# First four token tiles of an MLP layer in float32 on TensorE, and a new order of the start

## The chip, the cores and the metric

The kernel runs on one core of a Trainium2 chip. The metric is the device time of one execution in microseconds. TensorE (PE) multiplies matrices into PSUM, VectorE (DVE), ScalarE (ACT) and GpSimd (POOL) compute element by element, SyncE (SP) mostly issues transfers (DMA). Each engine works through its own queue in order.

## The reference

x is 2048 x 576 in float32, w1 576 x 4608, w2 4608 x 576. The result is the sum of x, a Fourier mixing of its layer norm, and a two-layer MLP of the same layer norm:

```python
xn = _layernorm(x, axis=-1)
# A: a = xn @ dft_hid_re.T ; b = xn @ dft_hid_im.T ; y = dft_seq_re @ a - dft_seq_im @ b
# B: h = maximum(xn @ w1, 0) ; y = h @ w2
return x + _A_ref(xn, A_dft_seq_re, A_dft_seq_im, A_dft_hid_re, A_dft_hid_im) + _B_ref(xn, B_w1, B_w2)
```

## The kernel before, in words

Tokens come in 16 tiles of 128, four to a group (`g` 0 to 3). The 4608 hidden features come in 9 blocks of 512; a block has two halves of w1 and of w2 (`i` 0 and 1), a half two slices of 128 features (`f`). TensorE works in f16: every float32 operand is split into a high f16 part and a low f16 remainder, and a product is made of high*high, high*low and low*high. From block 1 on, and in the Fourier part, products also go by a scheme of seven block products in place of eight; block 0 is plain.

The program has three stages: the MLP blocks 0 to 8, a transform along the hidden axis, and one along the sequence. Nothing is left to a scheduler: strings of words (`BLOCK0`, `BLOCK1`, `BLOCK`, ...) give the order, each word is one step for one engine, and within an engine the steps run in the order of their words. This document is on the start, block 0, whose words are:

- `lx:t` loads x tile t (L350), `lw:i` a half of w2 (L354), `load_w1_main` and `load_w1_rest` a half of w1 (L366, and L377 with L378), issued by SP or ScalarE. At most eight such transfers are under way: each takes one of eight semaphores in turn.
- `bn:t` and `ag:t`: row statistics of tile t on VectorE (L473, L477); `sq:a:b` on ScalarE and `ch:a:b` on VectorE: the factors of tiles a to b (L482, L489 to L493).
- `hi:t`: the high f16 part of the normalised tile into one of seven staging slots (ScalarE, L512 and L515); `xn:t`: the normalised tile in float32, in place, by ScalarE (`A`, L532) or VectorE (`V`, L534); `lo:t`: the low part (VectorE, or GpSimd `G`, L520 and L521); `T:t`: the staged tile transposed into `xT` by a transposing DMA that SP issues (L542).
- `th`, `tl`, `ch_`, `cl`: for tiles 0 and 1, the same transpose in f16 on TensorE (L553) with copies out of PSUM by ScalarE (L1114, L1115).
- Powers of two as scales: `ms` (ScalarE, L904) or `mx` (VectorE, L887) takes a maximum of w1; `pa` multiplies it across the partitions (TensorE, L434), `pb` reduces (VectorE, L437), `pc` spreads it (TensorE, L443), `pd` makes the scale (VectorE, L446 to L451). `sw`, `qm`, `qa` to `qd` do that for w2.
- `wh:f` and `wl:f`: high and low parts of w1 for two passes (ScalarE L921, VectorE L926 and L927); `uh`, `ul` the same for w2 (L1016, L1020).
- `p:t:i` (and `p0`): the first layer for tile t and half i, 28 f16 matmuls of 128 columns (L588), into a PSUM bank per slice. `f:n`: n idle matmuls (L1075).
- `oa`, `od`: ReLU, high part on ScalarE (L603), low on VectorE (L611). `m:g:k`: the second layer of block 0 for group g (TensorE, L850). `e`, `ad`: eviction and the transfer to DRAM. `P:g:f`: the first layer for a whole group g of 512 columns (L588).
- `ts`, `tu`, `tv`, `tw`: differences of tiles for the later blocks. `nx`, `na` to `nd`, `nh`, `nl`, `ns`: scale and split w1 of block 1.

The lines that a sentence can't say are the order of the start and the words' meaning in `act`:

```python
"th": lambda t: transposes_pe(t, HI, Q[0]), "tl": lambda t: transposes_pe(t, LO, Q[1]),
"p0": lambda f: piece(0, (f,), WK0), "p": lambda t, i: piece(t, (2 * i, 2 * i + 1)),
```

## Time and profile before

| | |
|---|---|
| median of 3 runs | 1224.66 us (1223.04 to 1225.59) |
| profiled execution | 1223.44 us |
| its span | 1221.7 us |
| TensorE busy | 1213.3 us, 99% of the span |
| VectorE, ScalarE, GpSimd busy | 1043.4, 726.5, 210.6 us |
| mean DMA rate | 144 GB/s |

Rows of the view in order of time have the start in us from the span's start, the length, the engine, the line, the operation, what is written and read, and a count; in brackets the engine's idle time just before and what ended it. In the view of groups a row ends with the busy time in us, the mean ns of one, and the idle time before. The view of stretches gives for each stretch its length, the busy time of PE, PEld (weight loads), DVE, ACT and POOL with counts, the granted TensorE clock, the busy share of the DMA engines and GB/s. The view of waits names who waited for whom: total us, times, longest. The 1.7 us between the span and the execution's time lie outside what the trace shows.

### The profile page before, as it was taken

The page shows a single profiled execution, that of the slowest core. Times are in us where ns is not written, and L with a number is a line of the kernel's source. Part 1 is how long each engine was busy: PE and PEld are TensorE (multiplying, and loading weights), DVE is VectorE, ACT ScalarE, POOL GpSimd, SP SyncE. Part 2 cuts the span into 40 slices and gives each one's busy share as a digit, 9 for nine tenths or more (in the row PEclk, how much of TensorE's full clock was granted, in tenths as well). Part 3 has the DMA queues.
Part 4 walks back from the last instruction along what each step waited for, and adds up shares of the span by engine and source line. Part 5 has one row for each costly group of instructions (what it writes and reads, how often), then busy time and mean ns, then how long its engine had stood idle before and what let it go on. Part 6 is the DMA issues. An engine that isn't in the chain of part 4 may idle for free.

```text
span 1221.7 us, 26201 instructions
## 1 busy us (share of the span) xinstructions
PE 1213.3 (99%) x10516; PEld 999.8 (82%) x10516; DVE 1043.4 (85%) x2004; ACT 726.5 (59%) x1251; POOL 210.6 (17%) x274
## 2 busy tenths in 40 slices
...
GB/s 234 227 170 197 158 133 181 148 155 151 164 140 169 152 146 175 134 144 150 148 120 153 140 186 166 113 98 66 157 150 136 134 79 47 92 158 182 141 133 35
DMA packets 127050, 175.97 MB, mean 144 GB/s; under 512 B 48336, under 2 KB 88784, under 8 KB 126928
## 3 DMA queue, kind: packets, MB, share of 16 engines
...
q10 hardware_dynamic: 560, 0.39, 0.1%
...
## 4 chain that ended last, share of the span: by engine, by line
PE 99%; DMA 1%; DVE 0%; POOL 0%; issue 0%; ACT 0%
PE bank L713 28%; PE bank L1483 27%; PE p L810 27%; PE bank L1397 8%; PE p L588 4%; PE p L850 4%; PE p L1075 1%; DMA raw_w<-in_w_dram 0%; DMA accs<-in_x_dram 0%; DVE st L473 0%; PE p L553 0%; DVE row L440 0%; POOL dbuf L521 0%; DVE o L1495 0%; PE p L434 0%
## 5 line engine op out<-in xcount | busy, mean ns | idle before, releaser
L810 PE MATMUL p<-w2s,h 128*128 128x288 f16 x2688 | 357.9, 286 | 0.0
L1483 PE MATMUL bank<-R,cs 128*128 128x288 f16 x2688 | 330.3, 286 | 0.0
L1483 PEld LDWEIGHTS <-cs 128*128 128x128 f16 x2688 | 263.0, 98 | 66.3
L810 PEld LDWEIGHTS <-h 128*128 128x128 f16 x2688 | 263.0, 98 | 61.7
L713 PEld LDWEIGHTS <-dbuf 128*128 128x128 f16 x1568 | 153.3, 98 | 21.1 <-issue 0.8
L713 PEld LDWEIGHTS <-wbuf 128*128 128x128 f16 x1568 | 153.4, 98 | 20.2
L1016 ACT ACTIVATE cs<-tb,sc_c 128x1024 f16<-128x1024 f32 x56 | 63.7, 1147 | 89.2 <-PE bank L1483 61.7
L713 PE MATMUL bank<-xT,wbuf 128*128 128x256 f16 x896 | 110.7, 273 | 0.0
L713 PE MATMUL bank<-xT,dbuf 128*128 128x256 f16 x896 | 110.2, 273 | 0.0
L835 POOL DMA_DIRECT2D spill<-dbuf x70 | 62.4, 933 | 159.5 <-DVE dbuf L828 117.0
L1020 DVE SCALAR_TENSOR_TENSOR cs<-tb,sc_c,cs 128x1024 f16<-128x1024 f32 x56 | 71.5, 1282 | 20.3 <-ACT cs L1016 19.6
L713 PE MATMUL bank<-accs,wbuf 128*128 128x256 f16 x672 | 86.9, 273 | 0.0
L713 PE MATMUL bank<-accs,dbuf 128*128 128x256 f16 x672 | 86.1, 273 | 0.0
L760 DVE TENSOR_TENSOR h<-s,h 128x1024 f16<-128x1024 f32 x64 | 77.4, 1217 | 1.7 <-ACT h L754 1.7
L1016 ACT ACTIVATE cs<-accs,sc_c 128x1024 f16<-128x1024 f32 x40 | 45.8, 1147 | 55.2 <-PE bank L1483 41.7
L754 ACT ACTIVATE h<-s 128x1024 f16<-128x1024 f32 x64 | 66.5, 1050 | 12.3 <-DVE s L751 12.3
L1246 ACT ACTIVATE f<-f 128x1024 f32<-128x1024 f32 x64 | 67.1, 1049 | 1.4 <-DMA f<-in_cre_dram 1.3
L835 POOL DMA_DIRECT2D spill<-wbuf x42 | 39.6, 942 | 148.8 <-DVE wbuf L828 120.5
L722 ACT ACTIVATE h<-accs 128x256 f16<-128x256 f32 x128 | 50.9, 409 | 23.8 <-DVE accs L737 21.7
L1020 DVE SCALAR_TENSOR_TENSOR cs<-accs,sc_c,cs 128x1024 f16<-128x1024 f32 x40 | 51.1, 1282 | 13.0 <-ACT cs L1016 12.7
L703 ACT ACTIVATE accs<-bank 128x256 f32<-128x256 f32 x97 | 36.9, 380 | 41.1 <-PE bank L713 20.0
L824 ACT ACTIVATE dbuf<-p,c_ub 128x576 f32<-128x576 f32 x61 | 45.0, 737 | 25.4 <-PE p L810 25.4
...
## 6 DMA issues: line engine op xcount, KB each, us to landing
spill<-dbuf POOLq DMA_DIRECT2D x80, 288.0 KB, 4.6
...
spill<-wbuf POOLq DMA_DIRECT2D x48, 288.0 KB, 5.6
raw_w<-in_w_dram SPq DMA_DIRECT2D x18, 576.0 KB, 4.8
...
```

The costliest lines, as they stand in the source:

```text
L588: nc.tensor.matmul(ps[:, cols], w1s[b, i // 2][:, i % 2 * 2 + h, y], xT[g][:, h * KC + z, cols], start=(n == 0), stop=(n == len(wk) - 1),)
L713: nc.tensor.matmul(ps, l, r, start=first and m == 0, stop=m == len(todo) - 1, skip_group_check=not first,)
L722: nc.scalar.activation(next(high_low(q)), SOURCE[q], AF.Relu)
L754: order["s"] = nc.scalar.activation(next(high_low(SUMS)), stage_of(slice(1, 5)), AF.Copy).ins
L760: order["lo"] = nc.vector.tensor_tensor(lo, stage_of(slice(1, 5)), hi, ALU.subtract).ins
L810: nc.tensor.matmul(ps[:, c], h[:, x, qa, c * P : (c + 1) * P], w[:, y, qb], start=first and i == 0 and j == 0, stop=i == NQ - 1 and j == 2 ...
L835: nc.gpsimd.dma_start(spill[g, row, col], sums[g, row, col], accum_op=ALU.add)
L1016: nc.scalar.activation(hi, src, AF.Copy, scale=s)
L1020: nc.vector.scalar_tensor_tensor(lo, src, s, hi, ALU.mult, ALU.subtract)
L1246: nc.scalar.activation(f, f, AF.Abs, scale=2.0**-10, accum_out=sums_c[:, n, q : q + 1])
L1397: nc.tensor.matmul(ps, x[:, k, c * P : (c + 1) * P], dsp[z][:, a, y], start=first and m == 0, stop=m == len(PASSES) - 1, skip_group_check= ...
L1483: nc.tensor.matmul(ps, w[:, a, RANK[k]], r[:, c, RIGHT[rq]], start=first and k == 0 and j == 0, stop=k == HK - 1 and j == 2, skip_group_ch ...
```

## The change

**Float32 for tiles 0 to 3.** In block 0 the first layer of the first four tiles no longer uses split operands. `tf:t` transposes the normalised float32 tile on TensorE (five matmuls with a float32 identity), `cm:t` and `cr:t` copy the result out of PSUM (four parts of 128 rows, and the rest of 64), and `pf:t:i` multiplies the raw w1 half with it in float32: two slices of five matmuls. Since the raw w1 isn't scaled, `sf:i` multiplies the finished PSUM banks by the scale, in place, before the ReLU. `th`, `tl`, `ch_`, `cl` and `p0` are gone. Tiles 0 to 3 still go through `hi` or the new `hj` (the same from `xn`), `lo` and `T` for later blocks, later than before.

**w1 by fewer transfers.** A half of w1 now takes three transfers in place of five. The first half goes through ScalarE's queue alone, x tiles 0 to 3 through SP.

**Order and engines.** `BLOCK0` and `BLOCK1` are written in a new order; only the first 84 idle matmuls are left. Some steps can go by VectorE that were ScalarE's (`hi`, `oa`, `wh`, `tu`, `sf`), and staging slots are handed out in another order of tiles.

```diff
+    def transposes32(t, main, rest):
+        for k in range(KM):
+            nc.tensor.transpose(main[:, k * P : (k + 1) * P], xns[t][:, k * P : (k + 1) * P], ident32)
+        nc.tensor.transpose(rest[:REM], xns[t][:, KM * P :], ident32)
...
+    def piece32(t, i):
+        for r in range(2):
+            w = raws["w1", 0, i]
+            ps = banks0[0][2 * i + r][:, t * P : (t + 1) * P]
+            for k in range(KM):
+                h, q = divmod(k, 2)
+                nc.tensor.matmul(ps, w[:, 2 * r + h, q], xt32[:, t, k], start=k == 0, stop=False)
+            nc.tensor.matmul(ps, w[:REM, 2 * r, 2], xt32[:REM, t, KM], start=False, stop=True)
+
+    def scaled(i, eng=nc.scalar):
+        ps = XY[i]
+        s = sc["w1", 0][:, i : i + 1]
...
     load_x(0)
...
-    for half in range(2):
-        eng = (nc.sync, nc.scalar)[half]
-        load_w1_main(0, 0, slice(half, half + 1), eng)
-        load_w1_rest(0, 0, half, eng)
-    for t in range(1, TG):
+    load_w1_main(0, 0, nc.scalar)
+    load_x(1)
+    load_w1_rest(0, 0, nc.scalar)
+    for t in range(2, TG):
         load_x(t)
-    load_w1_main(0, 1, slice(0, 2))
-    for half in range(2):
-        load_w1_rest(0, 1, half)
+    load_w1_main(0, 1)
+    load_w1_rest(0, 1)
...
 BLOCK0 = """
-bn:0 ag:0 sq:0:0 ch:0:0 bn:1 bn:2 bn:3 ag:2 hi:0 xn:0:A ms:0 ag:1 lo:0:G f:79 th:0 ag:3 mc:0
+f:79 bn:0 ag:0 lw:0 sq:0:0 ch:0:0 f:5 lw:1 xn:0:A bn:1 tf:0 ag:1 bn:2 sq:1:1 ch:1:1 xn:1:V cr:0:V
```

**Where instructions moved.** SP's queue at the start of the program, before: `accs` are x tiles, `raw_w_0` the halves of w1, then `raw_w_0_0_376` the first half of w2, and transposes (`xT`) ahead of x tiles 8 and 10.

```order
L350 DMA accs<-in_x_dram 128x576 x3
L366 DMA raw_w_0_1_149<-in_w_dram 128x4x256
L377 DMA raw_w_0_1_149<-in_w_dram 96x2x128
L378 DMA raw_w_0_1_149<-in_w_dram 32x2x128
L377 DMA raw_w_0_1_149<-in_w_dram 96x2x128
L378 DMA raw_w_0_1_149<-in_w_dram 32x2x128
L350 DMA accs<-in_x_dram 128x576 x4
L354 DMA raw_w_0_0_376<-in_w_dram 128x1152
L542 DMA_TRANSPOSE xT_134<-dbuf 128x10x128 x2
L350 DMA accs<-in_x_dram 128x576 x2
L354 DMA raw_w_0_1_693<-in_w_dram 128x1152
```

The same place of the changed kernel; `raw_w_0_0_269` and `raw_w_0_1_282` are the halves of w2, the two `accs` behind them tiles 8 and 10.

```order
L350 DMA accs<-in_x_dram 128x576 x4
L366 DMA raw_w_0_1_154<-in_w_dram 128x4x256
L378 DMA raw_w_0_1_154<-in_w_dram 96x4x128
L378 DMA raw_w_0_1_154<-in_w_dram 32x4x128
L350 DMA accs<-in_x_dram 128x576 x4
L354 DMA raw_w_0_0_269<-in_w_dram 128x1152
L354 DMA raw_w_0_1_282<-in_w_dram 128x1152
L350 DMA accs<-in_x_dram 128x576 x2
```

The second half of w2 and tiles 8 and 10 moved ahead of all transposes, right behind the first half of w2.

VectorE's queue around the statistics of tile 10 in block 0, before: `st_567` holds tile 10's, `st_570` tile 8's; the rows ahead are the end of the last split of w1 (`wl:3`) and a difference of tiles.

```order
L926 SCALAR_TENSOR_TENSOR wbuf<-raw_w_0_1_149,c_sw_210,wbuf 128x2x256
L927 SCALAR_TENSOR_TENSOR wbuf<-raw_w_0_1_149,c_sw_210,wbuf 32x2x128
L655 TENSOR_TENSOR accs<-accs 128x2x256
L655 TENSOR_TENSOR accs<-accs 128x2x32
L520 TENSOR_TENSOR dbuf<-accs,dbuf 128x2x32
L521 TENSOR_TENSOR dbuf<-accs,dbuf 128x2x256
L473 BN_STATS st_567<-accs 128x6 x2
L473 BN_STATS st_570<-accs 128x6 x2
```

The same work in the changed kernel: `st_391` holds tile 10's statistics, the copy behind it is `cr:3`, the reduction `pb:1`, then four aggregates and the first split of w1 (`wl:0`).

```order
L485 BN_STATS st_383<-accs 128x6 x2
L485 BN_STATS st_386<-accs 128x6 x2
L485 BN_STATS st_391<-accs 128x6 x2
L588 COPY xT_137<-p_0_1_3_185 64x128
L439 TENSOR_REDUCE top<-p_0_1_2_184 1x1
L489 BN_AGGR mv<-st_356 128x2
L489 BN_AGGR mv<-st_352 128x2
L489 BN_AGGR mv<-st_383 128x2
L489 BN_AGGR mv<-st_386 128x2
L962 SCALAR_TENSOR_TENSOR wbuf<-raw_w_0_0_153,c_sw_316,wbuf 128x2x256
L963 SCALAR_TENSOR_TENSOR wbuf<-raw_w_0_0_153,c_sw_316,wbuf 32x2x128
```

Tile 10's statistics moved from behind the last split of w1 to ahead of the first one, and ahead of the second power's reduction.

TensorE's queue around `pc:1` in the changed kernel; `p_0_0_0_180` and `p_0_0_1_181` are the banks of group 0, L575 and L576 transpose in float32 (`tf:3`), L1112 and L1113 are the float32 matmuls, L445 is `pc:1`.

```order
L436 MATMUL p_0_1_2_184<-ident,mb_1_372 1x128
L575 MATMUL p_0_1_1_183<-xT_136,accs 128x128 x4
L576 MATMUL p_0_1_3_185<-xT_136,accs 64x128
L1112 MATMUL p_0_0_0_180<-xT_137,raw_w_0_0_153 128x128 x4
L1113 MATMUL p_0_0_0_180<-xT_137,raw_w_0_0_153 128x128
L1112 MATMUL p_0_0_0_180<-xT_137,raw_w_0_0_153 128x128 x4
L1113 MATMUL p_0_0_0_180<-xT_137,raw_w_0_0_153 128x128
L445 LDWEIGHTS ones
L445 MATMUL p_0_1_3_185<-top,ones 128x1
L1112 MATMUL p_0_0_1_181<-xT_137,raw_w_0_1_154 128x128 x4
L1113 MATMUL p_0_0_1_181<-xT_137,raw_w_0_1_154 128x128
```

Before, idle matmuls (L1075) stood on both sides of `pc:1`; now work of the first layer stands ahead of it and behind it.

233 lines of the change are left out of this document (131 added, 102 removed).

## The prediction

> **What bounds the kernel now.** I read the page first, then TensorE's waits after the start, then TensorE in order of time.
>
> ```profile
> PE 1213.3 (99%) x10516; PEld 999.8 (82%) x10516; DVE 1043.4 (85%) x2004; ACT 726.5 (59%) x1251; POOL 210.6 (17%) x274
> PE bank L443 <- DVE row L440: 0.7, 1, 0.7
> 21.03 1.11 PE L1075 MATMUL p<-dbuf 128*128 128x128 f16 x17
> 21.98 11.11 PE L588 MATMUL p<-xT,wbuf 128*128 128x128 f16 x196
> 34.94 12.68 PE L588 MATMUL p<-xT,wbuf 128*128 128x128 f16 x224
> 47.45 11.92 PE L850 MATMUL p<-w2s,h 128*128 128x288 f16 x96
> ```
>
> TensorE is busy all through, but its first 22 us are mostly idle matmuls (L1075, `f`). The first matmul that counts starts at 21.98: the pieces (`p`) of the first layer for tiles 0 to 7, in two lots of 224. One takes 12.68/224 = 56.6 ns, a `p` word of 28 takes 1.585 us. At 47.45 the second layer begins (`m:0:0`), and from there to the end TensorE waits once, 0.7 us (the second row, the only one that the view of waits gives for it after 47 us). So a microsecond gained or lost ahead of `m:0:0` comes out at the end in full. What the change is worth is the new start of `m:0:0` against 47.45, and what becomes of that one wait.
>
> **The change, part by part: TensorE's own work.** Removed: all idle matmuls but 84, 20 f16 transposes, and the 224 f16 pieces of tiles 0 to 3 (12.7 us). Added: 80 float32 matmuls and 20 float32 transposes of 128 columns. No row has a float32 matmul. The kernel itself makes float32 products out of f16 halves, and high and low of both operands give at most four f16 products; so I count passes of 56.6 ns. Bounds: one pass from below; from above four, each with its weight load in the open:
>
> ```profile
> L588 PEld LDWEIGHTS <-wbuf 128*128 128x128 f16 x441 | 24.7, 98 | 0.1
> ```
>
> 4 x (98 + 56.6) = 618 ns. I take four passes whose loads hide behind the matmuls, as every load of the pieces does now (98 ns each, yet one piece every 56.6): 4 x 56.6 = 226 ns, so 18.1 us in all. That is 5.4 us more than the f16 pieces, but it needs no split weights, no scale and no transposing DMA, so it can run in the first 22 us. The transposes cost 5 x 56.6 to 5 x 226 ns a tile, 0.3 to 1.1 us.
>
> **How early float32 can start.** ScalarE's rows of before give the prices:
>
> ```profile
> 6.56 0.81 ACT L512 ACTIVATE dbuf<-accs,sh,r 128x512 f16<-128x512 f32 x1 [1.01 <-DVE sh L493]
> 7.67 0.85 ACT L532 ACTIVATE first_xn<-accs,sh,r 128x576 f32<-128x576 f32 x1
> 8.42 1.47 ACT L904 ACTIVATE wbuf<-raw_w 128x1536 f16<-128x1536 f32 x1
> 34.94 1.08 ACT L603 ACTIVATE h<-p 128x512 f16<-128x512 f32 x2 [0.93 <-PE p L588]
> ```
>
> Tile 0's factor is known at 6.56 as before, `xn:0` takes 0.85 (to 7.4), then come a deviation and the maximum of w1's first half (L904, with its accumulator about 1.65) ahead of `cm:0` (0.58 from PSUM, by L603): 10.0. The transposes of tile 1 stand in between on TensorE, so `pf:0:0` starts at about 10.9. Were nothing else in the way, float32 would be over at 10.9 + 18.1 + 2 us for transposes and powers = 31, and `m:0:0` would start at 31 + 12.7 = 43.7, a gain of 3.7.
>
> **What is in the way: x tile 10.** The new order loads both halves of w2 and then x tiles 8 and 10 right behind tiles 4 to 7, and VectorE's queue now holds the statistics of tile 10 ahead of `cr:3` and `pb:1`. TensorE's `pc:1` needs `pb:1`, and fifty float32 matmuls (`pf:0:1`, `pf:1:1`, `pf:3:0`, `pf:2:1`, `pf:3:1`) stand behind `pc:1`. When does tile 10 land?
>
> ```profile
> L354 SPq DMA_DIRECT2D raw_w<-in_w_dram x1: 328/328/328, 13.0 to 13.0; - x1
> DMA to landing us min/median/max: 5.3/5.3/5.3
> accs<-in_x_dram SPq DMA_DIRECT2D x12, 288.0 KB, 4.4
> raw_w<-in_w_dram SPq DMA_DIRECT2D x2, 576.0 KB, 5.1
> 12.00:14.00 2.00, 1.32 (x20) 1.15 (x21) 1.33 (x3) 0.83 (x2) 0.63 (x1) 1.00 1.01 281
> 24.00:26.00 2.00, 2.00 (x40) 2.00 (x38) 2.00 (x6) 2.00 (x5) 0.00 (x0) 1.00 1.00 302
> 26.00:28.00 2.00, 2.00 (x39) 2.00 (x37) 2.00 (x6) 2.00 (x5) 0.28 (x1) 1.00 0.99 384
> ```
>
> Before, the first half of w2 landed at 13.0 + 5.3 = 18.3, behind tiles 0 to 7 and w1; the bytes up to there are the same now. The last two columns are the DMA engines' busy share and GB/s: with a share of about 1.0 they move 281 to 384, so fewer, larger transfers can win little (I take 0.6 us, bounds 0 and 1.0). Tile 10 has 576 + 2 x 288 KB more ahead of it, itself included: 1.18 MB, at 384 to 281 GB/s 3.1 to 4.2 us; at 343, the mean of the last two rows, 3.4. So 18.3 - 0.6 + 3.4 = 21.1, bounds 20.4 and 22.5.
>
> **From tile 10 to `m:0:0`, on VectorE.** Starts of neighbours in order of time give each price:
>
> ```profile
> 15.84 0.57 DVE L534 TENSOR_SCALAR accs<-accs,mv,r 128x576 f32<-128x576 f32 x1
> 16.32 1.53 DVE L473 BATCH_NORM_STATS2 st<-accs 128x6 f32<-128x288 f32 x4
> ...
> 20.69 0.13 DVE L446 TENSOR_SCALAR half<-p 128x1 f32<-128x1 f32 x1
> ...
> 20.98 0.20 DVE L477 BATCH_NORM_AGGREGATE mv<-st 128x2 f32<-128x12 f32 x1
> 21.10 0.70 DVE L926 SCALAR_TENSOR_TENSOR wbuf<-raw_w,c_sw,wbuf 128x512 f16<-128x512 f32 x1
> ...
> 22.11 0.73 DVE L926 SCALAR_TENSOR_TENSOR wbuf<-raw_w,c_sw,wbuf 128x512 f16<-128x512 f32 x1
> ...
> 23.17 0.16 DVE L489 RECIPROCAL r<-u 128x4 f32<-128x4 f32 x1
> ...
> 24.05 0.74 DVE L926 SCALAR_TENSOR_TENSOR wbuf<-raw_w,c_sw,wbuf 128x512 f16<-128x512 f32 x1
> ...
> 27.64 0.20 DVE L520 TENSOR_TENSOR dbuf<-accs,dbuf 128x64 f16<-128x64 f32 x1
> ...
> 28.37 1.52 DVE L473 BATCH_NORM_STATS2 st<-accs 128x6 f32<-128x288 f32 x4
> 29.82 0.20 DVE L520 TENSOR_TENSOR dbuf<-accs,dbuf 128x64 f16<-128x64 f32 x1
> ...
> 31.28 0.66 DVE L973 CAST mb<-c_mw 128x2 bf16<-128x2 f32 x1
> 31.85 0.20 DVE L477 BATCH_NORM_AGGREGATE mv<-st 128x2 f32<-128x12 f32 x1
> ...
> 32.65 0.39 DVE L477 BATCH_NORM_AGGREGATE mv<-st 128x2 f32<-128x12 f32 x3
> 33.27 0.28 DVE L437 TENSOR_REDUCE top<-p 2x1 f32<-2x128 f32 x1 [0.22 <-PE p L434]
> ...
> 33.72 0.21 DVE L520 TENSOR_TENSOR dbuf<-accs,dbuf 128x64 f16<-128x64 f32 x1
> 35.04 0.16 DVE L446 TENSOR_SCALAR half<-p 128x2 f32<-128x2 f32 x1 [0.52 <-PE p L443]
> ...
> 36.28 0.21 DVE L520 TENSOR_TENSOR wbuf<-first_xn,wbuf 128x64 f16<-128x64 f32 x1
> ```
>
> Between tile 10 and the end of `wl:1` (w1's last split, which `p:6:0` needs) VectorE's queue holds: five tiles' statistics at 1.45/2 = 0.73 (3.63); four `wl` at 1.01 (4.04); two `lo` at 0.73 (1.46); one `ch` 0.88; `pd` 0.29; `pb` 0.28; `qb` 0.45; `qd` 1.24; `qm` 0.57; eight aggregates at 0.13 (1.04); one `xn` 0.48; one copy out of PSUM without a row of its own, between the 0.28 of the reduction and the 0.57 of the wide row, nearer the small one: 0.3. Sum 14.7. For waits on TensorE and ScalarE in between I add 1.2 (an estimate; the rows show 0.22 and 0.52 for two of them; bounds 0.3 and 2). So `wl:1` ends at 21.1 + 14.7 + 1.2 = 37.0.
>
> TensorE meanwhile: `pc:1` at 21.1 + 0.73 + 0.3 + 0.28 + 0.2 of hops = 22.6, then 50 x 0.226 = 11.3, 0.4 for the powers of w2, and `p:4:1` 1.6: 35.9. It waits 1.1 for `wl:1`. Seven `p` words of 1.585 follow (11.1) and end at 48.1. The transposing DMAs of tiles 4 to 7 are needed at 34.3, 37.0, 41.7 and 43.3 and stay ahead by my count of ScalarE's queue, tile 4 narrowly. For `od:0:1`, last of VectorE's work for `m:0:0`, I allow 0.2 (0 to 1). `m:0:0` starts at 48.3, 0.85 later than 47.45.
>
> **Given back at 107 us.** That one wait hangs between two matmuls of w1's power:
>
> ```profile
> 105.80 0.94 PE L713 MATMUL bank<-accs,dbuf 128*128 128x256 f16 x7
> 107.47 0.16 PE L443 MATMUL bank<-row,ones 2*128 2x2 bf16 x1 [0.73 <-DVE row L440]
> ```
>
> Seven products stand between them now, fourteen in the new order. Another seven (0.94) cover 0.73: gain 0.73 (0 if VectorE is late there).
>
> **Costed at nothing.** w1 of later blocks comes in 3 transfers in place of 5, which takes work off SP; TensorE waits for no transfer after 47 us. The in-place scaling (`sf`) and the new engines for single steps work beside a busy TensorE; if that cover is gone after 47 us, a wait of 1 to 3 us would show there, and that is inside the slower chance.
>
> **Sum.** +0.85 - 0.73 = +0.1 us, on the profiled execution 1223.44 + 0.1 = 1223.5. The median shown lies 1.2 above that execution, so 1224.8. With the bounds of tile 10 (-0.7, +1.4), of the waits (-0.9, +0.8) and of `od` (-0.2, +0.8), not all at one end, the likeliest case by itself runs from 1223.2 to 1227.2. A measurement here can tell about 0.2%, 2.4 us.
>
> **Rivals.** *Slower: float32's weight loads don't hide.* The rows show a load of 98 ns that hides because the next one proceeds behind a matmul; none shows it for 4-byte weights. At one load of 98 a pass, a matmul takes 392 ns. Float32 then runs without a break: 10.9 + 80 x 0.392 + 1 for transposes and powers + 12.7 = 56.0, that is 8.5 later, less 0.73: 1232.5. With transposes at 392 too it is 1235. It decides from where 50 matmuls behind `pc:1` outlast VectorE: 1.1 us of slack / 50 = 22 ns more, 248 ns; at 300 ns the cost is 2.6. For it: idle TensorE time is what the plan spends. Against: two of four passes could share a load.
>
> [...]
>
> *Faster: tile 10 comes early.* If DMA keeps 384 GB/s from the start, tile 10 lands near 18 and VectorE, not waiting, ends `wl:1` 3 us sooner; TensorE's own sum (43.7) and ScalarE's queue then allow `m:0:0` at about 45.3: -2.2 - 0.73, 1221.8. Against it: the 281 to 302 GB/s at a busy share of 1.0.
>
> *It does nothing that it says:* float32 starts at 11 but TensorE stands at `pc:1` and `wl:1` for what it saved. That is my forecast.
>
> **Chances.** Forecast 0.52; slower 0.34 (loads 0.28, new waits after 47 us 0.06); faster 0.14. Range 1221.8 to 1235: left out are loads dearer than the rival's (0.1) and a little below. The forecast's own case gives 0.48 within 0.2%, 0.04 slower; the faster one 0.12 faster, 0.02 within; the slower 0.32 slower and 0.02 within. So faster 0.12, same 0.52, slower 0.36.
>
> **What would show it.** Right: float32 matmuls about 226 ns apart, VectorE idle ahead of tile 10's statistics for 2 to 4 us, landing near 21; TensorE waiting at `pc:1` for VectorE and at `p:6:0` for `wl:1`; `m:0:0` at 48.3; no wait near 107. Wrong: float32 over 250 ns apart, or `m:0:0` before 46, or new waits of TensorE after 50 us.

## The result, and the profile after

The changed kernel takes 1241.66 us (median of 4 runs, 1240.48 to 1242.73), the kernel before 1225.08 (4 runs, 1223.04 to 1225.59): the ratio is 1.0138, 95% interval 1.0121 to 1.0156. The forecast of 1224.8 with a range from 1221.8 to 1235 was wrong. The profiled execution has a span of 1240.0, against 1221.7.

TensorE's busy row of the page of the changed kernel:

```profile
PE 1222.1 (99%) x10294; PEld 1001.7 (81%) x10294; DVE 1056.2 (85%) x2026; ACT 723.0 (58%) x1244; POOL 215.6 (17%) x277
```

The share is the same 99%; it doesn't show what happened. TensorE in order of time does (start, length, line; idle time before it in brackets, with what ended it). In the changed kernel L883 is the second layer, L620 the first, L436 and L445 the matmuls of a power, L746 and L843 block 1's products and its second layer:

```profile
11.87 1.16 PE L1112 MATMUL p<-xT,raw_w 128*128 128x128 f32 x8 [0.68 <-ACT xT L586]
...
50.53 6.04 PE L883 MATMUL p<-w2s,h 128*128 128x288 f16 x48
59.46 8.98 PE L883 MATMUL p<-w2s,h 128*128 128x288 f16 x72 [2.88 <-DVE wbuf L896]
69.53 6.20 PE L620 MATMUL p<-xT,wbuf 128*128 128x512 f16 x28 [1.10 <-issue]
...
81.98 0.16 PE L445 MATMUL pm<-top,ones 1*128 1x1 bf16 x1 [2.82 <-DVE top L439]
82.07 4.44 PE L883 MATMUL p<-w2s,h 128*128 128x288 f16 x24
...
117.76 0.22 PE L436 MATMUL bank<-ident,mb 128*2 128x128 bf16 x1 [0.47 <-DVE mb L1009]
...
119.54 0.17 PE L445 MATMUL bank<-row,ones 2*128 2x2 bf16 x1
...
128.74 1.26 PE L746 MATMUL bank<-accs,dbuf 128*128 128x256 f16 x7 [2.16 <-DVE s L772]
129.79 4.48 PE L883 MATMUL p<-w2s,h 128*128 128x288 f16 x24
...
150.92 3.22 PE L746 MATMUL bank<-xT,dbuf 128*128 128x256 f16 x28 [0.95 <-DVE s L784]
153.98 3.10 PE L843 MATMUL p<-w2s,h 128*128 128x288 f16 x24
```

`m:0:0` starts at 50.53, 3.1 later, and behind it six waits stand where before had one of 0.73. The rows that answer to three of these places in the kernel before (L443 at the end of w1's power, L434 at the start of w2's power, L810, block 1's second layer; in the changed kernel they are the rows at 81.98, 117.76 and 153.98):

```profile
71.72 0.17 PE L443 MATMUL pm<-top,ones 1*128 1x1 bf16 x1
...
105.65 0.22 PE L434 MATMUL bank<-ident,mb 128*2 128x128 bf16 x1
...
136.78 1.63 PE L810 MATMUL p<-w2s,h 128*128 128x288 f16 x12
```

These four places cut the way into stretches. The table has them for the two kernels and for the runs on which the explanation rests; every number is a difference of two starts in that run's profile.

| run | `m:0:0` starts | to w1's power | to w2's power | to block 1's second layer | which starts |
|---|---|---|---|---|---|
| before | 47.45 | 24.3 | 33.9 | 31.1 | 136.78 |
| after | 50.53 | 31.5 | 35.8 | 36.2 | 153.98 |
| h_before_after | 49.88 | 24.5 | 35.5 | 36.1 | 145.96 |
| h_after_before_2 | 50.55 | 33.6 | 33.9 | 31.7 | 149.85 |
| no_sums_of_group_0 | 50.66 | 26.1 | 35.5 | 34.3 | 146.58 |
| chain_early | 50.46 | 26.2 | 35.1 | 36.3 | 148.02 |
| block_1_order_before | 52.02 | 30.9 | 35.5 | 31.4 | 149.73 |

Each profile is one execution. In the five runs below that leave every step up to `m:0:0` as it is in the changed kernel, TensorE's first wait for tile 1 is 1.50 to 3.19 us long, the granted clock from 8 to 25 us 0.80 to 1.00, and `m:0:0` starts between 50.55 and 53.69. So a run's stretches behind `m:0:0` have to be read apart from its time.

The loss at 154 us is 3.1 + 7.2 + 1.9 + 5.1 = 17.2; 1.1 more comes behind it (18.3 in all between the two spans; the medians differ by 16.6). Three pieces of it are not waits. 24 matmuls of L883 take 4.44 and 4.48 in place of 3.10, twice. And about 0.8 of the 5.1 is no loss at that place: one product more (seven matmuls of L746, 147 in place of 140) stands ahead of the first L843 now. The granted clock (the column of 0.85 to 1.00, behind TensorE's busy time) around 82 us:

```profile
80.00:82.00 2.00, 0.02 (x1) 0.85 1.13 213
82.00:86.50 4.50, 4.50 (x26) 0.69 1.07 224
86.50:90.00 3.50, 3.50 (x20) 1.00 0.63 122
```

A wait of 2.8 us is followed by 4.5 us at 0.69 of the clock: it costs 1.3 us again.

### The profile page after: what moved, and what is told of

It reads as the page before. It is cut to its first block, busy times and chain, and to the rows that moved or that the text cites. A ratio compares the mean times of both kernels' runs of the same rounds, so it can differ in the third digit from the quotient of the medians.

```text
span 1240.0 us, 25723 instructions
## 1 busy us (share of the span) xinstructions
PE 1222.1 (99%) x10294; PEld 1001.7 (81%) x10294; DVE 1056.2 (85%) x2026; ACT 723.0 (58%) x1244; POOL 215.6 (17%) x277
## 3 DMA queue, kind: packets, MB, share of 16 engines
q1 hardware_dynamic: 99216, 122.25, 33.9%
## 4 chain that ended last, share of the span: by engine, by line
PE 87%; DVE 7%; DMA 3%; ACT 1%; issue 1%; SPq 1%; POOL 0%; DVEq 0%; ACTq 0%; POOLq 0%
PE bank L1535 27%; PE bank L746 25%; PE p L843 25%; PE bank L1449 8%; DMA raw_w<-in_w_dram 1%; PE p L883 1%; DMA accs<-in_x_dram 1%; DVE w2s L1056 1%; DVE c_mf L920 1%; PE p L1112 1%; DMA xT<-wbuf 1%; SPq L699 0%; DVE h L759 0%; ACT dbuf L532 0%; DVE wbuf L542 0%
## 5 line engine op out<-in xcount | busy, mean ns | idle before, releaser
L843 PE MATMUL p<-w2s,h 128*128 128x288 f16 x2688 | 358.0, 286 | 0.4
L843 PEld LDWEIGHTS <-h 128*128 128x128 f16 x2688 | 262.9, 98 | 63.2 <-issue 1.3
L746 PEld LDWEIGHTS <-dbuf 128*128 128x128 f16 x1568 | 153.4, 98 | 23.5 <-issue 3.5
L746 PEld LDWEIGHTS <-wbuf 128*128 128x128 f16 x1568 | 153.4, 98 | 20.2
L746 PE MATMUL bank<-xT,wbuf 128*128 128x256 f16 x896 | 110.9, 273 | 0.0
L746 PE MATMUL bank<-xT,dbuf 128*128 128x256 f16 x896 | 109.9, 273 | 0.9 <-DVE s L784 0.9
L746 PE MATMUL bank<-accs,dbuf 128*128 128x256 f16 x672 | 86.8, 273 | 2.2 <-DVE s L772 2.2
L1056 DVE SCALAR_TENSOR_TENSOR cs<-tb,sc_c,cs 128x1024 f16<-128x1024 f32 x56 | 71.5, 1282 | 20.1 <-ACT cs L1052 19.8
L746 PE MATMUL bank<-accs,wbuf 128*128 128x256 f16 x672 | 86.9, 273 | 0.0
L1056 DVE SCALAR_TENSOR_TENSOR cs<-accs,sc_c,cs 128x1024 f16<-128x1024 f32 x40 | 51.1, 1283 | 13.3 <-ACT cs L1052 12.8
```

The source lines that it names most:

```text
L746: nc.tensor.matmul(ps, l, r, start=first and m == 0, stop=m == len(todo) - 1, skip_group_check=not first,)
L843: nc.tensor.matmul(ps[:, c], h[:, x, qa, c * P : (c + 1) * P], w[:, y, qb], start=first and i == 0 and j == 0, stop=i == NQ - 1 and j == 2 ...
L1056: nc.vector.scalar_tensor_tensor(lo, src, s, hi, ALU.mult, ALU.subtract)
```

## The experiments

**Which half of the new order costs?** The first four runs separate the start from what follows it.

```diff
 ... xn:11:A lo:8:V m:0:0
-m:0:1 ag:15 tv:0:0:V sq:12:15 ch:12:15 lo:11:G oa:1:1 tw:0:0 od:1:1 T:9 e:0:0:V ...
+tv:0:0:V tw:0:0 tu:0:2 ag:15 od:1:2 lo:11:G tv:0:2:V oa:1:1 m:0:1 e:0:0:V ...
```

> The changed kernel's steps up to and with m:0:0 (float32 start, new loads, new order), and from there on the remaining steps in the order and on the engines of before. Theory ORDER (the new order behind m:0:0 costs by itself): what is left of the loss is the later m:0:0, 50.53 against 47.45, so 1225.1 + 3.1 = 1228.2; eight steps that before had done by m:0:0 are still to be done, which may cost one short wait, so 1227.5 to 1231. TensorE stands still for under 2 us between 51 and 152 us (10.4 after the change) and its clock does not fall at 82 and at 129 us. Theory LATE (the waits come only because everything after the float32 stage starts 3 us late): the waits stay whatever the order, 1238 to 1242.

1241.39, ratio 1.0133 (1.0112 to 1.0154). It seemed to speak for LATE, but nearly all of TensorE's idle time was one wait: 8.2 us in front of `e:0:0`, behind a chain that I had put there myself (`tv:0:0`, its transposing transfer, `tu:0:2`, `tv:0:2`). The run was made again below.

The opposite half, on the kernel before:

```diff
 ... tv:0:2:V ag:13 oa:1:1 m:0:0
-m:0:1 e:0:0:V lo:8:V ts:1:1:V ...
+L1:0 L1:1 T:10 lo:8:V m:0:1 sq:12:15 ch:12:15 od:1:1 T:9 e:0:0:V ad:0:0 ...
```

> The other half: the steps of before up to and with m:0:0 (no float32, the old loads), and from there on the remaining steps in the changed kernel's order and on its engines. Theory ORDER: TensorE's idle time of 10.4 us between 50 and 152 us, less the 0.73 that before had, and about 3 us of lowered clock come back although nothing is late: 1225.1 + 10 to 14 = 1235 to 1239, with VectorE's eviction of m:0:0 waited for and the clock lowered near 79 and 126 us. Theory LATE: with m:0:0 at 47.45 the new order has the slack that it was written for, 1224.4 to 1227 (0.73 less for the filled wait at 107 us).

1230.07, ratio 1.0053 (1.0035 to 1.0071): between the two. Its profile on TensorE says where:

```profile
49.88 15.06 PE L858 MATMUL p<-w2s,h 128*128 128x288 f16 x120
...
74.34 0.17 PE L443 MATMUL pm<-top,ones 1*128 1x1 bf16 x1
...
121.04 1.65 PE L721 MATMUL bank<-accs,dbuf 128*128 128x256 f16 x7 [2.37 <-DVE s L747]
```

Behind the old start the new order has no wait from `m:0:0` up to w1's power; it has the wait of block 1 (2.37, against 2.16 in the changed kernel) in full. The stretch of +7.2 needs the new start, that of +5.1 does not. (This execution took 1234.79, the longest of six: its clock lay at 0.66 from 10 to 20 us, and `m:0:0` came 2.4 later than in the kernel before, with the same start.)

```diff
-... hi:14:V ... xn:15:A ... tu:1:1:V ... lo:14:V ... oa:2:0:V ... tu:1:2:V ... oa:2:2:V ... e:1:2:V ... oa:2:3:V ... tv:3:1:G
+... hi:14 ... xn:15:V ... tu:1:1 ... lo:14:G ... oa:2:0 ... tu:1:2 ... oa:2:2 ... e:1:2:A ... oa:2:3 ... tv:3:1:V
```

> The changed kernel with ten of its engine choices behind m:0:0 put back to those of before (tu:1:1, tu:1:2, oa:2:0, oa:2:2, oa:2:3, hi:14 and e:1:2 from VectorE to ScalarE, lo:14 to GpSimd, xn:15 and tv:3:1 to VectorE); the order stays. Theory ENGINES (VectorE is given steps that stand behind transposing transfers): the wait of 2.82 at 81.98 goes, and with it the fall of the clock that makes 24 matmuls take 4.44 in place of 3.10; the waits of 1.1 at 69.53 and of 2.16 at 128.74 may go too: 1241.7 - 2.8 - 1.3 = 1237.5, down to 1232 if all three go. Theory PLACES (the places of the steps in VectorE's row cost it, not the engines): 1240 to 1243.

The wait at 82 and the low clock behind it went (1.00 from 70 to 90 us), and block 1's second layer started 3.6 sooner in the profile (150.37); the time stayed at 1241.49 (ratio 1.0140, 1.0119 to 1.0161; runs from 1239.6 to 1244.2). The other waits stayed. So in this order that one wait hangs on the engines, but no change of the time is shown.

```diff
-            for k in range(KM):
+            for k in range(KM // 2):
```

> The changed kernel with two of the four full row blocks of w1 left out of its float32 products (6 matmuls of 10 are left in a pf; the first layer of tiles 0 to 3 is only partly computed). This takes 32 x 0.272 = 8.7 us out of TensorE's float32 stage, more than the 6 us by which it was dearer than forecast. Theory LATE: m:0:0 starts at 47.5 or before and the waits behind it go: 1225 or less. Theory ORDER: m:0:0 starts earlier by 1 to 4 us (VectorE ends wl:1 at 38.9 in the changed kernel, of which about 2 us were waits for TensorE's powers), but VectorE's row reaches e:0:0 at 56 to 58.6 whatever m:0:0 does, so the wait in front of it grows by what m:0:0 gains, and the other waits stay: 1237 to 1241.

1244.39, ratio 1.0155 (1.0131 to 1.0179). With 8.7 us of float32 gone, `m:0:0` started at 51.14, no sooner. TensorE first waited 2.5 us for tile 1 and then ran at half the clock until 25 us:

```profile
15.00:20.00 5.00, 5.00 (x20) 0.50 1.03 395
20.00:25.00 5.00, 5.00 (x19) 0.50 0.76 280
```

and later it waited 1.07 for the last split of w1, which VectorE ended at 41.1. Both theories failed on the size. With the clock at half, the run doesn't show what float32 alone costs; it shows that VectorE's row can bound `m:0:0` too.

**Single waits.** Four runs took one thing each out of the stretch behind the start.

```diff
-m:0:0 m:0:1 ag:15 tv:0:0:V sq:12:15 ch:12:15 lo:11:G oa:1:1 tw:0:0 od:1:1 T:9 e:0:0:V
+m:0:0 m:0:1 e:0:0:V ag:15 tv:0:0:V sq:12:15 ch:12:15 lo:11:G oa:1:1 tw:0:0 od:1:1 T:9
```

> The changed kernel with one step moved: VectorE's eviction e:0:0 from its place behind fifteen VectorE instructions to the place directly behind the issue of m:0:1. Theory QUEUE (the 2.88 at 59.46 is only the place of e:0:0 in VectorE's row): VectorE reaches it at 52.1, waits till m:0:0 is done at about 53.6, and frees the bank at 54.5, before TensorE needs it at 56.6: the wait goes, 1241.7 - 2.9 = 1238.8; the fifteen instructions behind it come 1 to 2.4 us later, so of the wait of 1.1 at 69.53 and 2.82 at 81.98 up to 2 may be added back: 1237.5 to 1241. Rival BACKLOG (VectorE has more work in this stretch than TensorE gives it time for; a step moved forward only moves the wait): the sum of TensorE's idle time from 50 to 100 stays at 6.8 to 7.5 and the time at 1241 to 1243.

1243.02 (1.0166, 1.0148 to 1.0184): the wait shrank to 0.31, and one of 3.10 for VectorE's `od` (L646) came at 71. So a wait did move, as BACKLOG says, though TensorE's idle time from 50 to 100 us fell to 3.8, from 6.8. The time doesn't tell the two apart: in the profile TensorE had waited 3.19 for tile 1, its clock lay at 0.54 from 10 to 15 us, and `m:0:0` started at 53.68, 3.2 later than in the changed kernel.

```diff
-... hj:0 bn:10 pa:1 ... qm:0 bn:8 pf:0:1
+... hj:0 pa:1 ... qm:0 bn:8 bn:10 pf:0:1
```

> The changed kernel with the statistics of tile 10 (bn:10) moved in VectorE's row from ahead of cr:3 and pb:1 to behind those of tile 8. VectorE waited 2.53 there for tile 10's transfer. Theory X10 (that wait pushes VectorE's whole row up to wl:1, m:0:0 and e:0:0): cr:3 and pb:1 come 2 to 2.5 earlier, wl:1 ends near 37 in place of 38.99, m:0:0 starts at 49 to 49.5 in place of 50.53, the wait at 59.46 falls from 2.88 to 1.5 to 2.4: 1241.7 - 1 to 2 = 1239.7 to 1240.7, at most 1238.5. Rival FLOAT32 (TensorE's own sum sets m:0:0): m:0:0 stays within 0.4 of 50.5 and the time at 1241 to 1242.5, whatever VectorE gains.

1245.00 (1.0172, 1.0153 to 1.0191), worse than either theory. TensorE's clock lay at 0.50 from 15 to 25 us in the profile, VectorE then waited 4.56 for the transposes of tile 3, and `m:0:0` started at 56.54. What tile 10 costs by itself stays open.

```diff
-lo:1:G ... lo:4:G ... lo:5:G ... lo:3:G ... lo:0:G ... lo:2:G ... ts:0:2:G ts:0:3:G ... lo:9:G ... lo:10:G ... ts:1:0:G ... lo:11:G
...
-        nc.gpsimd.memset(st[:, :, 2, RH : 2 * RH], 0.0)
+        nc.gpsimd.memset(st[:, :, 2:], 0.0)
```

> The changed kernel without the twelve steps (lo and ts) that GpSimd does ahead of e:0:0: the low halves of tiles 0 to 5 and 9 to 11 stay zero, and some sums of rows are left out, so that part of the product is missing. VectorE's row and places stay. Between 36 and 58.6 us nine VectorE instructions took longer than their like elsewhere, each beside a GpSimd instruction: L963 1.38 against 0.47, L1056 1.38 against 0.81, L503 1.01 against 0.16, L542 1.77 against 0.68, L541 1.06 and 0.71 against 0.20, L502 0.91 against 0.16: together 5.4 us. Theory SHARED (the two engines stand in each other's way): they take 0.47, 0.81, 0.16, 0.68, 0.20 and 0.16, wl:1 ends 0.9 sooner, VectorE reaches e:0:0 by 54, the wait at 59.46 goes and m:0:0 comes up to 0.9 earlier: 1241.7 - 2.9 - 0.9 = 1238, down to 1235 if the later waits shrink too. Rival DATA (these instructions wait for their inputs or for transfers): they keep their lengths, 1240 to 1242.5.

Three of VectorE's instructions in the changed kernel:

```profile
37.61 1.38 DVE L963 SCALAR_TENSOR_TENSOR wbuf<-raw_w,c_sw,wbuf 32x256 f16<-32x256 f32 x1
...
42.67 1.01 DVE L503 SCALAR_TENSOR_TENSOR u<-r,u 128x4 f32<-128x4 f32 x1
...
53.67 1.77 DVE L542 TENSOR_TENSOR dbuf<-accs,dbuf 128x512 f16<-128x512 f32 x1
```

The same three without GpSimd's steps, and ahead of them one that stood beside GpSimd's longer memsets (9.10 to 15.27 us):

```profile
10.42 5.16 DVE L560 TENSOR_SCALAR accs<-accs,mv,r 128x576 f32<-128x576 f32 x1
...
43.54 0.47 DVE L963 SCALAR_TENSOR_TENSOR wbuf<-raw_w,c_sw,wbuf 32x256 f16<-32x256 f32 x1
...
47.49 0.16 DVE L503 SCALAR_TENSOR_TENSOR u<-r,u 128x4 f32<-128x4 f32 x1
...
56.30 0.68 DVE L542 TENSOR_TENSOR dbuf<-accs,dbuf 128x512 f16<-128x512 f32 x1
```

SHARED is shown for the lengths: without GpSimd's steps the three take 0.47, 0.16 and 0.68, in place of 1.38, 1.01 and 1.77. The wait for `e:0:0` went too, but `m:0:0` came 5.9 later, which gave VectorE that much more time ahead of it. The time was 1241.98 (1.0148, 1.0133 to 1.0164) all the same, since VectorE's L560, 5.16 long beside the memsets that fill the place of the missing halves, ended at 15.6, and tile 1's transposes, which wait for it, began at 15.63, behind a wait of 6.94. `m:0:0` started at 56.41, yet the end came no later (this kernel leaves out twelve steps). That VectorE instruction, begun at 10.42, ended only behind the last of the row of memsets (15.27) and not behind the next one.

```diff
 ... lo:8:V m:0:0 m:0:1
-ag:15 tv:0:0:V sq:12:15 ch:12:15 lo:11:G oa:1:1 tw:0:0 od:1:1 T:9 e:0:0:V ...
+e:0:0:V tv:0:0:V tw:0:0 tu:0:2 ag:15 od:1:2 lo:11:G tv:0:2:V oa:1:1 ts:1:1:V ...
```

> Again the changed kernel up to m:0:0 and the order and engines of before behind it, but with the eight steps that before had already done by m:0:0 put behind e:0:0 (in the first such run they stood ahead of it, and TensorE waited 8.2 us for e:0:0 behind a chain of two of them and a transposing transfer). Theory ORDER: e:0:0 is done when TensorE needs it, and what is left is the later m:0:0 (3.1, or 5 to 6 if the clock falls in the first 25 us as in that run) and the wait of 0.73 that before has too: 1227.5 to 1231. Rival BACKLOG (VectorE comes out of the start so far behind that any order waits): TensorE's idle time between 50 and 152 us is over 5 us and the time 1235 to 1241.

1239.73 (1.0133, 1.0118 to 1.0148): BACKLOG. `e:0:0` was in time, but now ScalarE's eviction (L894) was 7.07 late, and its own row shows why:

```profile
62.74 0.83 ACT L532 ACTIVATE wbuf<-accs 128x512 f16<-128x512 f32 x2 [9.26 <-DMA accs<-wbuf]
```

ScalarE stood 9.26 us at `tu:0:2`, which needs the place that the transposing transfer `tw:0:0` (accs<-wbuf) frees, and the evictions stand behind it in its row. The last stretch was as short as before (31.7): that part belongs to the order of block 1.

**The chain of tiles 0 to 3.** The waits of that run and of the changed kernel point to one chain: sums of the four tiles (`ts`), high halves (`tu`), low halves (`tv`), transposing transfers (`tw`). SyncE's row in the kernel before, and then in the changed one (L662 and L695 are `tw`):

```profile
38.04 1.33 SPq L662 DMA_TRANSPOSE accs<-wbuf  x1
...
40.21 1.26 SPq L662 DMA_TRANSPOSE accs<-wbuf  x1
```

```profile
55.21 2.20 SPq L695 DMA_TRANSPOSE accs<-wbuf  x1
57.51 1.50 SPq L568 DMA_TRANSPOSE xT<-dbuf  x1
59.11 1.43 SPq L695 DMA_TRANSPOSE accs<-wbuf  x1
```

Before had both `tw` issued by 41.5, ahead of `m:0:0`; now the second comes at 59.1. Is SyncE's row the cause, and does such a delay suffice?

```diff
-T:0 p:4:1 T:1
+p:4:1
...
-hi:8 T:3 ul:1:0 bn:13 od:0:3 p:5:1 T:2
+hi:8 ul:1:0 bn:13 od:0:3 p:5:1
...
+    nc.vector.memset(xT[0], 0.0)
```

> The changed kernel without the four transposing DMAs T:0 to T:3 (block 1 then reads zeros for tiles 0 to 3, so that part of the product is missing). The runs before this one moved or took away each wait behind m:0:0 in turn, and the time stayed within 1237 to 1245: something that all of them leave in place sets the time. Theory TRANSPOSES: SyncE's row, where a transposing DMA takes 1.3 to 3.0 us to issue, one behind the other. Before has two of them for tiles 0 to 3 (T:2, T:3; tiles 0 and 1 go through TensorE) at 17.9 to 22; the change has four, at 41.8 to 53, so the sums' transposes (tw:0:0, L695) start at 55.2 in place of 38.0, and every tu, tv, nx and eviction that stands behind them in ScalarE's and VectorE's rows is late. Without the four SyncE gets 4 x 1.4 to 2.4 = 6 to 9 us back: tw:0:0 starts at 46 to 50, the waits of 1.1 at 69.53 and 2.82 at 81.98 go (with 1.3 of lowered clock), the first L843 behind 136 us starts at 147 to 150 in place of 154: 1234 to 1238. Rival VECTORE (VectorE's row is the bound): tw:0:0 moves, the time does not: 1240 to 1243.

1243.25 (1.0152, 1.0120 to 1.0183): no gain. `tw` did not come sooner (56.21 and 60.56): SyncE was free from 54.1, and `tv` on VectorE ended at 56.15. Here it waited for its halves, not for SyncE. But this doesn't clear SyncE: VectorE's row ran 4.1 us later than in the changed kernel (`wl:1` ended at 43.05 in place of 38.99), behind a clock of 0.69 and 0.63 from 10 to 20 us. In the changed kernel `tv` ended at 52.09 and SyncE issued transfers of w1 up to 55.1, so there SyncE held the first `tw` for 3.1 us. What that costs stays open.

```diff
-lx:14 tw:0:0 lx:13 tw:0:1
+lx:14 lx:13 D:0 D:1 D:2 D:3 tw:0:0 tw:0:1
+        "D": lambda k: nc.sync.dma_start_transpose(xT[3][:, :, k * P : (k + 1) * P], stages[:, 5 + k % 2] ...),
```

> The kernel before with four more transposing DMAs between T:7 and tw:0:0 on SyncE, of halves that lie ready, into a place that is written over later; x tile 13's load stays ahead of them. Nothing else changes. Theory TRANSPOSES: tw:0:0 and all that SyncE issues behind it come 6 to 8 us later (44 to 46 in place of 38.0), the tu behind it hold ScalarE and VectorE, and TensorE gets waits between 50 and 110 us that sum to 3 to 8: 1227.5 to 1233. Rival VECTORE: these transfers have 6 us and more of slack: 1224 to 1225.5.

1236.95 (1.0097, 1.0081 to 1.0114), more than expected. SyncE, and TensorE in the same run:

```profile
40.30 7.96 SPq L1116 DMA_TRANSPOSE xT<-dbuf  x4
48.38 3.69 SPq L662 DMA_TRANSPOSE accs<-wbuf  x2
```

```profile
48.49 6.04 PE L850 MATMUL p<-w2s,h 128*128 128x288 f16 x48
56.63 7.71 PE L850 MATMUL p<-w2s,h 128*128 128x288 f16 x48 [2.09 <-DVE wbuf L863]
...
70.59 8.05 PE L588 MATMUL p<-xT,wbuf 128*128 128x512 f16 x28 [6.25 <-DMA xT<-dbuf]
```

A `tw` that comes 10 us later, in the kernel before, is enough for two waits of 8.3 us together and a lowered clock (0.86, 0.84 and 0.78 in the three tens from 50 to 80 us, 1.00 without the four). Part of it is SyncE's later transfers (the 6.25 is for a tile's own transpose), so this run does not single out the chain.

```diff
-lo:1:G ag:6
+lo:1:G lo:0:G ag:6
...
-lx:12 lx:13 qd:0
+lx:12 lx:13 T:1 T:0 qd:0
...
-wl:1 pf:3:1 lo:0:G sf:1
+wl:1 pf:3:1 sf:1
...
-od:0:2 T:0 p:4:1 T:1
+od:0:2 p:4:1
```

> The changed kernel with the transposing DMAs of tiles 1 and 0 moved forward on SyncE, from behind T:7 to behind the last load of x (issued at 19.9), and lo:0 on GpSimd from behind lo:3 to behind lo:1, so that the halves of both tiles are ready at 18; the same work in all. Theory TRANSPOSES: SyncE is idle from 20 to 28.8 in the changed kernel; the two use that time and give back 2 x 1.4 to 2.4 = 3 to 5 us at 42 to 53, so tw:0:0 starts at 51 to 52.5 and the time falls by 2 to 4: 1237.5 to 1240. Rival VECTORE: no change, 1240 to 1243.

1242.41 (1.0137, 1.0099 to 1.0175; runs from 1235.5 to 1245.6): no gain shown. As in no_T0_to_3, VectorE's row ran 4.1 us later in the profile (`wl:1` ended at 43.06) and `tw` waited for it: 55.7 and 60.0. `m:0:0` started at 53.68, 3.2 later than in the changed kernel, yet this execution took 1240.08, against 1241.82.

```diff
-                nc.tensor.matmul(ps, w[:, 2 * r + h, q], xt32[:, t, k], start=k == 0, stop=False)
+                nc.tensor.matmul(ps, w[:, 2 * r + h, q], xt32[:, a:b, k], start=k == 0, stop=False)
...
-pf:0:0 pa:0 pb:0 tf:2
+pa:0 pb:0 tf:2
```

> The changed kernel with its float32 products made for two tiles at a time: 40 matmuls of 256 columns in place of 80 of 128, so half the weight loads for the same columns; a word for two tiles takes the place of the second of two words. Theory LOADS (a float32 matmul of 128 columns takes 0.272 and not 4 x 0.0566 = 0.226 us because each of its two recorded loads of 191 ns shows beyond what its matmul hides): a word for two tiles takes 4.5 to 5 us, against 2 x 3.01 now, and the float32 stage ends 3 to 5 us sooner, as far as VectorE lets it. Rival PASSES (the streaming of float32 itself is slower than four f16 passes): 5.8 to 6.1 us. For the whole time, theory TRANSPOSES: 1240 to 1243 either way, since what sets it is not TensorE's start; if the float32 stage sets it: 1237 to 1239.

(`a:b` are the two tiles.) 1240.57 (1.0129, 1.0114 to 1.0145). Half a word, five matmuls, for one tile in the changed kernel (22.73 to 24.23), then half a word for two tiles in this run (19.51 to 22.06):

```profile
22.73 1.16 PE L1112 MATMUL p<-xT,raw_w 128*128 128x128 f32 x8
23.82 0.48 PE L1113 MATMUL p<-xT,raw_w 64*128 64x128 f32 x2
24.23 1.16 PE L1112 MATMUL p<-xT,raw_w 128*128 128x128 f32 x8
```

```profile
19.51 1.99 PE L1113 MATMUL p<-xT,raw_w 128*128 128x256 f32 x8
21.44 0.70 PE L1114 MATMUL p<-xT,raw_w 64*128 64x256 f32 x2
22.06 0.22 PE L436 MATMUL p<-ident,mb 128*1 128x128 bf16 x1
```

Each matmul is recorded as two. Eight records take 23.82 - 22.73 = 1.09 at 128 columns, 136 ns each, and 21.44 - 19.51 = 1.93 at 256, 241 ns each: 105 ns for 128 columns more, by my estimate two passes of 52.5 (an f16 matmul of 128 columns takes 56.6 in the kernel before), and 31 ns left over. A word for two tiles takes 2 x 2.55 = 5.1, against 2 x 3.01: nearer to LOADS (4.5 to 5) than to PASSES (5.8 to 6.1). That the 31 ns don't depend on the columns and are the load is argued from these two lengths, not shown. It brought nothing here, since float32 began at 15.17 in place of 11.87, waiting for the second tile, and ran at a clock of 0.62 from 15 to 20 us.

The next four are on the chain, block 1's order, the clock at the start and the transfers of w1.

```diff
+zs:0
...
-ts:0:0:V ... ts:0:1:V ... ts:0:2:G ts:0:3:G tu:0:1 ... tu:0:0 ... tv:0:1:V tw:0:1 ... tv:0:0:V ... tw:0:0
...
-tu:0:3 ... tv:0:3:G ... tu:0:2 ... tw:0:3 ... tv:0:2:V tw:0:2
...
+        "zs": lambda _: nc.scalar.activation(accs[:, 3 * XW : 3 * XW + XSW], eps.to_broadcast([P, XSW]), AF.Copy, scale=0.0),
```

> The changed kernel without the sums of tiles 0 to 3 for block 1 (ts:0, tu:0, tv:0 and tw:0, sixteen steps on VectorE, GpSimd, ScalarE and SyncE; zeros stand in their place, and block 1's products of these tiles are partly missing). By the runs so far the loss of 17.2 at the first L843 has three parts: m:0:0 later (+3.1), from m:0:0 to the first L445 of w1's power 31.5 in place of 24.3 (+7.2), and from the power of w2 to L843 36.2 in place of 31.1 (+5), the rest 1.9. The stretch from m:0:0 to L445 is short (24.5) with the new order behind the old start, and long (33.6) with the old order behind the new start, and delaying tw:0:0 by 10 us in the kernel before cost 12.6. Theory CHAIN: the new start leaves no room for this chain of sums, which before had run by 40 us; it now falls behind m:0:0, where tu and tv stand in ScalarE's and VectorE's rows waiting for its transposing transfers. Without it the stretch is 24.3 to 27 and the time 1241.7 - 4.5 to 7 (and the lowered clock at 82) = 1233.5 to 1237. Rival LOAD (not this chain, but all that VectorE has to do there): the stretch stays over 28.5 and the time over 1238.

1238.38 (1.0112, 1.0081 to 1.0143). w1's power now follows `m:0:0`, which stands where it was, by 26.1 us, not 31.5, as CHAIN says. The median lies above CHAIN's 1237: this profile is of the execution of 1234.13, and two of the four took over 1241.

```profile
50.66 6.11 PE L883 MATMUL p<-w2s,h 128*128 128x288 f16 x48
...
76.76 0.16 PE L445 MATMUL pm<-top,ones 1*128 1x1 bf16 x1 [0.16 <-DVE top L439]
```

```diff
 BLOCK1 = """
-0m:2:2 0od:3:1 0oa:3:3 0rw:1 0od:3:3 0od:3:2 0rw:0 0rm:0 p:0:0:1 f:0:0:1:V ...
+p:0:0:1 0tv:3:0:G 0m:2:2 0rw:1 0oa:3:3 0rw:0 f:0:0:1:V 0od:3:1 0od:3:2 0rm:0 ...
```

> The changed kernel with the order and the engines of before from the end of block 0's table on (its last steps of block 0 and all of block 1). Theory BLOCK1 (the third part, +5, is the new order of block 1: 2.16 and 0.95 of waits for VectorE's s, a clock that falls after the longer one, and seven products more): the stretch from w2's power to L843 goes from 36.2 to 31 to 32, and the wait of 0.73 between the power's two matmuls comes back: 1241.7 - 5 + 0.7 = 1237.4, 1236 to 1238.5. Rival LATE (these waits follow from the lateness ahead): they stay, 1240 to 1243.

1238.45 (1.0119, 1.0100 to 1.0137). BLOCK1: the last stretch went from 36.2 to 31.4 (0.8 of it is the product that stands behind L843 again), with waits of 0.42 and 0.32 in place of 2.16 and 0.95; the 1.45 at its start still counts to the stretch ahead.

```profile
118.32 0.22 PE L436 MATMUL bank<-ident,mb 128*2 128x128 bf16 x1 [1.45 <-DVE mb L1009]
...
139.27 0.93 PE L746 MATMUL bank<-accs,dbuf 128*128 128x256 f16 x7 [0.32 <-DVE s L772]
...
149.73 1.63 PE L843 MATMUL p<-w2s,h 128*128 128x288 f16 x12
```

```diff
-tf:0 ag:1 ... tf:1 lx:8
+tf:0 f:20 ag:1 ... tf:1 f:8 lx:8
```

> The changed kernel with 20 idle matmuls between the transposes of tiles 0 and 1 and 8 behind those of tile 1, where TensorE waits 1.5 to 3.2 and 0.6 to 1.0 us. In the profile of the changed kernel the granted clock stays at 1.00 up to 80 us; in seven of the runs made from it, those with a first wait of 1.8 us and more among them, it lies at 0.50 to 0.78 between 10 and 20 us, and m:0:0 starts 42 to 46 us behind the first float32 transposes of tile 1 in place of 40.1. Theory CLOCK: with the idle matmuls the clock stays at 1.00 in the start, m:0:0 starts 39.8 to 40.3 behind those transposes; the time is that of the changed kernel's own undisturbed start, 1240 to 1242, and spreads less. Rival: the clock falls all the same, or the idle matmuls delay the start by over 0.5 us: 1242 to 1245.

1240.13 (1.0132, 1.0114 to 1.0150). The clock stayed at 1.00 up to 60 us, although a wait of 2.37 was left, and `m:0:0` followed tile 1's transposes by 40.4. This agrees with CLOCK, but less_float32's and this run's waits differ by 0.15 only, so it does not show that the idle matmuls did it.

```diff
     def load_w1(b, i):
-        load_w1_main(b, i, slice(0, 2))
-        for r in range(2):
-            load_w1_rest(b, i, r)
+        load_w1_main3(b, i)
+        load_w1_rest3(b, i)
```

> The kernel before with one part of the change alone: w1 of block 1 and of the later blocks comes in 3 transfers in place of 5; block 0's stays as it was. All theories: SyncE gets two issues of 0.43 to 1.4 us less for each half of w1, TensorE waits for none of these transfers, so no change: 1223.5 to 1225.5. Against it would be over 2.4 us either way.

(The two functions are the changed kernel's loads.) 1224.26 against 1224.06, ratio 0.9999 (0.9990 to 1.0008): nothing, as costed.

**The same work, the chain moved forward.** The last two runs keep the whole computation.

```diff
+cm:2:A hj:2 hj:3 lo:2:V lo:3:V bn:10 cr:3:V
+lo:1:G lo:0:G ... lx:13 T:1 T:0 T:2 T:3 wl:0 ts:0:0:V ts:0:1:V ts:0:2:G ts:0:3:G
+xn:5:A tu:0:1 tu:0:0 ... wl:1 tv:0:1:V tv:0:0:V ... T:7 tw:0:1 tw:0:0
```

> The changed kernel's computation whole, with the chain of tiles 0 to 3 moved forward into times in which the changed kernel's engines wait: hj:2 and hj:3 into ScalarE's wait of 2.1 at 16.3, lo:2 and lo:3 into VectorE's wait of 2.5 for tile 10, lo:0 behind lo:1 on GpSimd, T:0 to T:3 behind the last load of x on SyncE (idle from 20 to 28.8), ts:0 ahead of VectorE's wait of 1.8 at 27.1, tu:0:0 and tu:0:1 to the places of hj:3 and hj:2, tv behind wl:1, tw behind T:7. Theory CHAIN: tw:0:0 starts at 41 to 44 in place of 59, the stretch from m:0:0 to the first L445 of w1's power falls from 31.5 to 26 to 28.5 as without the chain, and the time by 3 to 6: 1235.5 to 1239. m:0:0 itself stays (50 to 52), since float32 and VectorE's row up to wl:1 stay. Rival LOAD: the same work at other places only moves the waits, 1239.5 to 1243.

1236.82, ratio 1.0113 (1.0096 to 1.0130), 4.8 below the changed kernel. `m:0:0` stands where it was; SyncE and TensorE:

```profile
20.46 20.01 SPq L568 DMA_TRANSPOSE xT<-dbuf  x8
41.27 3.82 SPq L695 DMA_TRANSPOSE accs<-wbuf  x2
```

```profile
50.46 0.42 PE L883 MATMUL p<-w2s,h 128*128 128x288 f16 x2
...
57.45 8.98 PE L883 MATMUL p<-w2s,h 128*128 128x288 f16 x72 [0.22 <-DVE wbuf L896]
...
76.61 0.16 PE L445 MATMUL pm<-top,ones 1*128 1x1 bf16 x1 [0.72 <-DVE top L439]
```

With `tw` at 41 to 45 the wait of 2.88 is 0.22, that of 2.82 is 0.72, that of 1.10 is gone. So 5.3 of the 7.2 come from the place of the chain and of the steps that feed it, not from their work.

```diff
-tf:0 ag:1
+tf:0 f:24 ag:1
...
-m:0:0 m:0:1 ag:15
+m:0:0 m:0:1 e:0:0:V ag:15
...
 BLOCK1 = """
-0m:2:2 0od:3:1 0oa:3:3 0rw:1 ...
+p:0:0:1 0tv:3:0:G 0m:2:2 0rw:1 ...
```

> The same, and with it the order of before from the end of block 0's table on (which took about 3 us off by itself), e:0:0 directly behind m:0:1, and 24 and 8 idle matmuls in the two first waits of TensorE. If the parts add up (CHAIN): 3 to 6 and 3 to 4 off 1241.7 and 1 for e:0:0: 1230.5 to 1235; what is left against before is m:0:0 at 50.5 to 52 in place of 47.45 and 2 to 4 of waits. Rival LOAD: 1237 to 1240, the block 1 part alone.

1236.91 (1.0101, 1.0086 to 1.0116): the parts do not add up. Block 1's stretch fell to 32.4, but the one ahead of w1's power rose to 30.1 again, with a wait of 3.10 for VectorE's `od` at 67.9, the same as in e00_forward; `e:0:0` moved forward is in both, but no run shows that it is the cause. No version beat the kernel before.

## Why the prediction was wrong

- **Float32's price** was put at 226 ns a matmul; it is 301 on average (3.01 us a word of ten), between my bounds of 56.6 and 618. 128 columns more add 210 ns, near the 226 of four f16 passes; the 62 ns left over would be loads that do not hide in full, by my estimate from the lengths at 128 and 256 columns; no run shows it apart. That would be the slower rival's mechanism; at 300 ns it gave 2.6 more, so `m:0:0` at 50.9, and it starts at 50.53. The rival's own price, one load of 98 ns a pass and 392 ns in all, is not what the trace has: 272 ns for 128 rows, with only two loads recorded for a matmul (191 ns each on average). (That rival's time takes 1 us for transposes and powers where the first sum takes 2; with 2 it is 1233.5, not 1232.5.)
- **Tile 10** was right: forecast 21.1, VectorE took it up at 21.39 after a wait of 2.53; `pc:1` was to come at 22.6 and came at 22.64. That match is partly luck: float32 began at 11.87 in place of 10.9, behind waits of 1.52 for `xn:1` and 0.68 for `cm:0`, and at its dearer price TensorE itself reached `pc:1` only at 22.5. What I put behind it, TensorE standing at `pc:1` and `p:6:0`, was not: float32 took so long that it hardly waited there. The end of `wl:1` was 38.99 in place of 37.0, with waits of 1.81 and 0.80 for TensorE's powers, which stood behind the dearer float32.
- **The wait at 107 us** went, as said (L445 at 119.54 without one); 0.47 for `mb` came ahead of it. It stood in the power of w2 of block 1, not of w1 as I wrote.
- **The step that failed** is "Costed at nothing": the new order behind `m:0:0` and the new engines were to work beside a busy TensorE, at 1 to 3 us if that cover were gone, with a chance of 0.06. It cost 14.1 of the 17.2 us: 7.2 up to w1's power, 1.9 up to w2's, 5.1 in block 1 (0.8 of it the product that only moved ahead). Of this term the fewer transfers of w1 did cost nothing (0.9999 by themselves), and no wait of TensorE shows between the scaling in place (38.12) and `m:0:0`. The cover was read from a trace in which the first two transposes of the sums, `tw:0:0` and `tw:0:1`, were issued at 38.0 and 40.2. I followed VectorE's row up to `wl:1` alone, and did not ask what the new start pushes behind `m:0:0`. The two word tables showed it: `tw:0:0` stands ahead of `m:0:0` in the one and behind it in the other (59.1 in the trace), since the low halves of these tiles, which have to be taken before the sums overwrite the tiles, come later. And of block 1's new order I looked at one place, the wait at 107. That the place of the chain makes most of the 7.2, and the order of block 1 most of the 5.1, is what chain_early and block_1_order_before show.
- **"A microsecond ahead of `m:0:0` comes out at the end in full"** held for a TensorE that never waits. It fell with the waits: in T_early, which does the whole work, `m:0:0` was 3.2 later than in the changed kernel and the profiled execution no longer (1240.08, 1241.82).

What stays open: how the 3.1 at `m:0:0` divides between float32 and VectorE's row; how much of the 7.2 is GpSimd in VectorE's way or SyncE's row, since no_gpsimd_steps and chain_early each take the wait of 2.88 nearly or wholly away; and why chain_early and the old order of block 1 don't add up.
